# Natural token order, whole-tile stores, singly gated weights, early filler matmuls and a new order list in a gated-attention and channel-mixer kernel

## The chip, the cores and the metric

The kernel runs on one core of a Trainium2 chip. The metric is the device time in microseconds (us) of one execution. PE is TensorE, DVE VectorE, ACT ScalarE, POOL GpSimd, and SP the queue that issues loads and stores. An eviction is a copy of a result out of PSUM, the memory that PE writes to. Executions of one kernel differ here by up to 2.5% (171.99 to 176.32 us in one set of rounds), so runs marked slow (over 1.5% above the fastest of the same kernel) are left out, and ratios are taken over fast runs alone.

## The reference, cut to what matters

```python
# attention: batch 4, 8 heads, 768 tokens, head size 48; a decayed state per head
for t in range(S):
    state = alpha[:, :, t, :, None] * state + np.einsum('bhd,bhe->bhde', k[:, :, t], v[:, :, t])
    y[:, :, t] = np.einsum('bhd,bhde->bhe', q[:, :, t], state)
# then, on x = y as (4, 768, 384)
xt = x.transpose(0, 2, 1)
h = np.maximum(xt @ w_tok1, 0.0) @ w_tok2          # token mixing, 768 -> 256 -> 768
u = x + h.transpose(0, 2, 1)
h2 = np.maximum(u @ w_ch1, 0.0) @ w_ch2            # channel mixing, 384 -> 1536 -> 384
return (u + h2).astype(np.float32)
```

## The kernel before

The attention is cut into 12 steps of 256 tokens (three for each batch). A step loads alpha, k, q and v (`at`, `kt`, `qt`, `vt`, 393 KB each), builds decays by a cumulative sum of logarithms on PE, scales k and q with them (`pkk`, `pkq`), transposes both, and adds an intra-chunk part (`G`, mask, `y`) to a part from the carried state. After three steps a batch goes through the mixer: first and second token matmuls (weights `wt`), the add `u`, transposes, 24 groups of first channel matmuls with ReLU (`c1`, `rt`; weights `wc`), 24 groups of second channel matmuls (`c2`), the output add `o`, and the store. Batches overlap.

Partition p of a step holds the two tokens 2p and 2p+1, so attention comes out with even tokens ahead of odd ones. The kernel before leaves them so: the token weights are loaded and permuted to match, and each output tile is stored in two halves with rows 2 apart.

```python
    def wt2perm(self, e, stage):                       # on POOL, after the second token weight has landed
        d = self.wt2.rearrange("p k (c s t) -> p k c s t", s=2, t=64)
        s = self.natural(stage).rearrange("p k (c t s) -> p k c s t", s=2, t=64)
        for k in range(NDT):
            self.copy(e, d[:, k], s[:, k])

    def store(self, o, b, i, last):
        dst = self.out[b, i * 128 : (i + 1) * 128, :].rearrange("(t s) d -> s t d", s=2)
        for h, q in enumerate((self.nc.sync, self.nc.scalar if last else self.nc.sync)):
            q.dma_start(dst[h], self.t(o)[64 * h : 64 * h + 64, :])

    # ... weights wait for one fixed load each:
    weight("wt2", 0, 1, 786432, gates[NB - 1]["kt"], -69990.0, stage)   # k of step 2
    weight("wc2", p, 2, 1179648, gates[NB]["qt"], -69970.0 + p)         # q of step 3
```

Every operation is put on its engine in the place that a long list gives it (`ORDER`, found by a search outside the kernel); the last letter names the engine (t PE, s ACT, v DVE, g POOL, y SP):

```python
ORDER = """
ld_at0y ln0s cumw0t ld_at1y ln1s cumw1t ld_qt0y E0s IE0s ld_at3y qq0g trq0t ld_kt0y kk0v trk0t ln13s ld_qt1y
# ... cut: 839 entries in all
"""
```

Of the kernel before, what the change touches and what calls it, by code (L numbers as in the profile page):

```python
# [23 lines left out]
class Op:  # L24
    __slots__ = ("name", "eng", "prio", "preds", "vals", "emit", "mode", "idx", "start", "end", "on", "dma", "port",
                 "occ")
# [37 lines left out]
class Plan:  # L64
# [51 lines left out]
    def decode(self):  # L116
        free = {"PE": 700.0, "ACT": 700.0, "DVE": 3200.0, "POOL": 3200.0, "SP": 700.0}
# [7 lines left out]
        dma_in, dma_w, slow = 2400.0, 0.0, []  # L125
# [5 lines left out]
        for o in self.order:  # L131
            e = o.on
            occ, lat = o.eng[e]
            r = free[e]
            for p in o.preds:
                if not (e == "PE" and p.on == "PE"):
                    r = max(r, p.end)
            for v in o.vals:
# [42 lines left out]
            if o.dma is not None:  # L181
                kind, dur, lead, tail = o.dma
                if kind == "w":
                    s = max(st + lead, dma_w)
                    dma_w = s + dur
                    slow.append((s, dma_w))
                    o.end = dma_w + tail
                else:
                    dma_in = self.landed(max(st + lead, dma_in), dur)
                    o.end = dma_in + tail  # L190
            for v in o.vals:
# [20 lines left out]
W_SHARE = 0.18  # L212
B, H, S, D = 4, 8, 768, 48
HD, DT, DCH = 384, 256, 1536
NB = 3
# [13 lines left out]
def build(g):  # L229
# [6 lines left out]
    gates = {}  # L236


    def attention(n):
# [7 lines left out]

        at, kt, qt, vt = V("at"), V("kt"), V("qt"), V("vt")
        ld = {}
        for v, nm in ((at, "at"), (kt, "kt"), (qt, "qt"), (vt, "vt")):  # L250
            ld[nm] = P.op(f"ld_{nm}{n}", {"SP": (450.0, 450.0)}, -90000.0 + 10 * n, writes=[v],
                          emit=lambda e, v=v, nm=nm: g.load(nm, v, b, k), dma=("i", IN_NS, 1100.0, 650.0))
        gates[n] = ld
# [3 lines left out]
        if n in WIDE:  # L257
            lnp = O("ln", act(768, True), 0, writes=[la], reads=[at], preds=[ld["at"]], emit=lambda e: g.lnw(la, at))
            cb = V("pair")
            cum = O("cumw", pe([384] * 4 + [2] * 8), 2, writes=[cb], reads=[la], preds=[lnp],  # L260
# [4 lines left out]
        else:  # L265
# [22 lines left out]
        trk = O("trk", pe([64] * 8), 8, writes=[bk], reads=[pkk], preds=[kk], emit=lambda e: g.tr(bk, pkk), mode="R")  # L288
        trq = O("trq", pe([64] * 8), 8, writes=[bq], reads=[pkq], preds=[qq], emit=lambda e: g.tr(bq, pkq), mode="R")
        evk = O("evk", either(dve(1024, True), act(1024)), 9, writes=[tpk], reads=[bk], preds=[trk],  # L290
                emit=lambda e: g.trev(e, tpk, bk))
        evq = O("evq", either(dve(1024, True), act(1024)), 9, writes=[tpq], reads=[bq], preds=[trq],
                emit=lambda e: g.trev(e, tpq, bq))
        gtm = V("gtm")
        masks = []
        for sl in range(2):
            gp = V("pair")
            G = O(f"G{sl}_", pe([128] * 4), 10 + sl, writes=[gp], reads=[tpk, tpq], preds=[evk, evq],
                  emit=lambda e, sl=sl, gp=gp: g.gmm(gp, tpk, tpq, sl), mode="G")
            masks.append(O(f"mask{sl}_", dve(1024), 12 + sl, writes=[gtm], reads=[gp], preds=[G],  # L300
                           emit=lambda e, sl=sl, gp=gp: g.mask(gtm, gp, sl)))
        nst = 2 if k < NB - 1 else 1
        kp = V("pair")
        KO = O("K", pe([48] * 8), 9.5, writes=[kp], reads=[pkk, vb], preds=[kk, vc],
# [16 lines left out]
        yi = O("y", pe([48] * 16), 14, writes=[yp], reads=[gtm, vb], preds=masks + [vc],  # L321
# [17 lines left out]
    def weight(nm, piece, npart, bytes_, gate, prio, stage=None):  # L339
        o = P.op(f"ldw_{nm}{piece}", {"POOL": (850.0, 850.0)}, prio, preds=[gate] if gate else [],  # L340
                 writes=[stage] if stage else [], emit=lambda e: g.weight(nm, piece, gate, stage), dma=("w", bytes_ / 286.0, 2600.0, 800.0))
# [3 lines left out]
    def mixer(b):  # L345
# [4 lines left out]
        for m in range(NDT):  # L350
            bank, ht = V("one"), V("ht")
            if b == 0:
                prev = None
                for kc in range(NS):
                    o = P.op(f"t1_{b}_{m}_{kc}", pe([384]), m0 + 900 * m * sc + kc, writes=[bank], reads=[x[kc][0]],
                             preds=[x[kc][1], wl[("wt1", 0)], wl[("wt1", 1)]] + ([prev] if prev else []),
                             emit=lambda e, m=m, kc=kc, bank=bank: g.tok1(bank, m, kc, x[kc][0]))
                    prev = o
            else:
                prev = P.op(f"t1_{b}_{m}", pe([384] * 6), m0 + 900 * m * sc, writes=[bank], reads=[v for v, _ in x],  # L360
                            preds=[o for _, o in x] + [wl[("wt1", 0)], wl[("wt1", 1)]],
# [36 lines left out]
        for i in range(NS):  # L398
# [3 lines left out]
            for q4 in range(4):  # L402
                pp = []
                for mc in range(3 * q4, 3 * q4 + 3):
# [8 lines left out]
            last = b == B - 1 and i == NS - 1  # L413
            P.op(f"st_{b}_{i}", {"SP": (600.0 if last else 1180.0, 600.0)}, m0 + (16800 + 1950 * (i + 1)) * sc + hold, reads=[o_], preds=[oo],
                 emit=lambda e, i=i, o_=o_, last=last: g.store(o_, b, i, last), dma=("i", OUT_NS, 1000.0, 700.0))
# [3 lines left out]
    for p in range(2):  # L419
        weight("wt1", p, 2, 393216, gates[NB - 1]["kt"], -70000.0 + p)  # L420
    stage = V("ut")
    weight("wt2", 0, 1, 786432, gates[NB - 1]["kt"], -69990.0, stage)
    wl[("wt2", 0)] = P.op("wt2p", either({"POOL": (1700.0, 1750.0)}, {"ACT": (1650.0, 1750.0)}), -69000.0, port=True, preds=[wl[("wt2", 0)]],
                          reads=[stage], emit=lambda e: g.wt2perm(e, stage))
    for p in range(3):
        weight("wc1", p, 3, 786432, gates[NB - 1]["kt"], -69980.0 + p)
    for n in range(NB, B * NB):
        attention(n)
    for p in range(2):
        weight("wc2", p, 2, 1179648, gates[NB]["qt"], -69970.0 + p)  # L430
# [5 lines left out]
ENGINES = {"t": "PE", "s": "ACT", "v": "DVE", "g": "POOL", "y": "SP"}  # L436
ORDER = """
ld_at0y ln0s cumw0t ld_at1y ln1s cumw1t ld_qt0y E0s IE0s ld_at3y qq0g trq0t ld_kt0y kk0v trk0t ln13s ld_qt1y
ld_vt0y IE1s E1s qq1v ld_kt1y kk1g ld_vt1y evq0v evk0s G0_0t G1_0t Et1s mask0_0v vb0s K0t Et0s mask1_0v trq1t
evq1s trk1t vb1g s0_0v evk1v sa1_0v y0t ia0t fe0s G1_1t mask1_1v sm1_0g G0_1t mask0_1v ib0t x0_0v ld_at2y ln2s  # L440
cumw2t K1t E2s ld_kt2y ld_at4y P3g P4g sa0_1v x1_0s y1t ld_qt2y qq2v sm0_1v IE2s kk2v trq2t ld_vt2y vb2s ia1t
fe1s ib1t Et2s x0_1v trk2t evk2v evq2s sa1_1v lnP4s K2t G0_2t G1_2t r13s ldw_wt10g mask0_2v x1_1s ld_qt3y
ldw_wt11g t1_0_1_0t mask1_2v ldw_wt20g ld_kt3y sm1_1g q0r3g sa0_2v cum4t t1_0_0_0t t1_0_1_1t t1_0_0_1t sm0_2v
t1_0_0_2t lnP3s t1_0_0_3t k0a3v ldw_wc12g cum3t y2t ia2t fe2v ib2t x0_2s t1_0_1_2t t1_0_1_3t ldw_wc10g x1_2v
t1_0_0_4t t1_0_0_5t ht_0_0v wt2pg IE3s t1_0_1_4t E4s t1_0_1_5t ht_0_1s E3s kk3v ld_vt3y vb3s t2_0_1t u_0_1v
t2_0_0t u_0_0v IE4s ln14s ld_qt4y t2_0_5t u_0_5v ldw_wc11g t2_0_3t u_0_3v trk3t evk3s t2_0_4t u_0_4v t2_0_2t
u_0_2v ld_at5y up_0_0t ut_0_0s qq3g trq3t evq3v up_0_2t up_0_1t ut_0_1v K3t s0_3v sa1_3v G1_3t G0_3t ut_0_2s
c1_0_0_1t mask0_3v mask1_3v c1_0_0_0t c1_0_8_0t sm1_3g rt_0_0_0s r14s q0r4g ld_qt5y ld_kt4y c1_0_1_0t rt_0_1_0s
c1_0_9_1t c1_0_9_0t rt_0_0_1v c1_0_11_0t rt_0_9_1v rt_0_11_0s c1_0_3_1t c1_0_4_1t P5v lnP5s y3t ln15s qq4g ia3t
fe3s c1_0_7_1t c1_0_2_0t ld_vt4y rt_0_3_1v rt_0_4_1v r15s rt_0_7_1v rt_0_2_0s cum5t ld_kt5y ib3t rt_0_8_0s  # L450
ldw_wc20g IE5s E5s x1_3s k0a4v kk4v x0_3v c1_0_10_1t c1_0_10_0t rt_0_10_0s c1_0_11_1t c1_0_6_1t ldw_wc21g trk4t
evk4s rt_0_10_1v ld_at6y trq4t c1_0_5_1t rt_0_6_1v rt_0_11_1v c1_0_4_0t k0a5g c1_0_3_0t rt_0_3_0s rt_0_4_0s
q0r5v kk5g rt_0_5_1v evq4v c1_0_2_1t rt_0_2_1v c1_0_8_1t rt_0_8_1v qq5v c1_0_7_0t rt_0_7_0s rt_0_9_0s c1_0_6_0t
rt_0_6_0s c1_0_1_1t rt_0_1_1v trk5t evk5v trq5t c1_0_5_0t G1_4t vb4s K4t sa0_4v c2_0_2_0t sm0_4g mask1_4v
rt_0_5_0s sa1_4v sm1_4v c2_0_4_0t c2_0_4_1t ld_vt5y vb5g evq5s ld_at9y G0_5t G0_4t mask0_4v c2_0_3_0t mask0_5v
c2_0_1_0t c2_0_2_1t c2_0_2_2t c2_0_3_1t G1_5t K5t sa0_5v c2_0_3_2t c2_0_4_2t ld_at7y ln17s r17s c2_0_1_1t
c2_0_1_2t c2_0_1_3t ln16s P6v mask1_5v lnP6s P7v sm0_5v y5t o_0_1v y4t ld_qt6y ia4t ld_at8y P8g ld_qt7y ld_vt7y
lnP7s ia5t fe5v fe4v P9g c2_0_3_3t o_0_3v ib5t x1_5v ib4t x1_4v cum7t c2_0_2_3t q0r7v ld_vt6y x0_5s c2_0_4_3t
cum6t E7s ld_kt7y x0_4s t1_1_1t r16s lnP9s ld_kt6y ht_1_1v st_0_3y st_0_1y t1_1_0t c2_0_0_0t c2_0_5_0t ln18s
IE7s E6s ht_1_0s t2_1_5t t2_1_3t q0r6v ld_qt9y ld_at11y ld_vt8y qq7v IE6s ln19s o_0_2v qq6v t2_1_1t u_1_3v  # L460
u_1_1v c2_0_5_1t c2_0_5_2t t2_1_0t st_0_2y t2_1_2t c2_0_0_1t vb6g c2_0_5_3t u_1_2v up_1_1t k0a6g kk6g t2_1_4t
u_1_0v up_1_0t r19s u_1_5v lnP8s u_1_4v c2_0_0_2t k0a7g c2_0_0_3t up_1_2t ut_1_1s vb7s kk7g ut_1_0v c1_1_2_0t
o_0_4v o_0_5v rt_1_2_0v K6t ut_1_2v ld_vt9y trq7t evq7s c1_1_0_0t s0_6v o_0_0v sa1_6v c1_1_11_0t rt_1_11_0v
rt_1_0_0v c1_1_4_0t rt_1_4_0v c1_1_3_1t ld_kt8y ld_at10y rt_1_3_1s c1_1_1_0t rt_1_1_0v st_0_0y c1_1_8_0t
rt_1_8_0v trq6t evq6s trk6t evk6v trk7t c1_1_5_1t rt_1_5_1s sm1_6v evk7v c1_1_6_0t K7t G1_6t vb8s sa0_7v sm0_7v
c1_1_3_0t c1_1_1_1t rt_1_1_1s ld_kt10y rt_1_6_0v sa1_7v c1_1_6_1t rt_1_6_1s r18s P10g sm1_7g mask1_6v cum9t IE9s
cum8t c1_1_7_1t IE8s rt_1_7_1s c1_1_5_0t ld_kt11y E9s c1_1_9_0t ld_qt8y q0r8g E8s ln110s c1_1_4_1t c1_1_7_0t
# [416 lines left out]
```

## Time and profile before

| stretch of the profiled execution | us | what limits it |
|---|---|---|
| front, to the first channel matmul | 38.3 | loads and weights, one after another |
| dense part, to the last output add | 132.9 | PE, idle for 1.3 us |
| tail, last output add and last store | 4.2 | one store after one add |
| span | 175.4 | |
| time of a run | 178.06 median (177.62 to 178.57) | |

The slices, the stretches and the chain of waits are shown and read in the prediction. The stretches are read thus: us of the stretch, then busy us (and instructions) of PE, PEld (weight load), DVE, ACT and POOL, then the granted clock, the share of the DMA engines and GB/s. One more view of the kernel before is needed later: what DVE and PE waited for between 90 and 110 us (who waited for whom; total us, times, longest):

```profile
DVE o L831 <- DMA out_dram<-o: 2.8, 2, 2.2
PEld L634 <- DVE o L831: 1.2, 1, 1.2
PE ps L634 <- DVE o L831: 0.8, 1, 0.8
```

Output adds stand waiting for a free output buffer, which an earlier store still holds, and PE stands waiting for the adds.

### The profile page before, as it was taken

How to read it: one execution, taken by the hardware profiler on the slowest of the kernel's cores; microseconds unless marked ns; L12 is line 12 of the kernel's file. 1: busy time of each engine (PE TensorE's matmuls, PEld its weight loads, DVE VectorE, ACT ScalarE, POOL GpSimd, SP SyncE). 2: the span in 40 equal slices, each digit the busy share in tenths (PEclk: the TensorE clock that was granted, in tenths of full speed). 3: DMA queues.
4: the chain of work that ended last, by engine and by line, in shares of the span. 5: the costliest groups of instructions: out<-in, count | busy, mean ns of one | idle time of the engine just before them, and what ended most of it. 6: DMA issues, size and time to landing. Idle time of an engine off the chain costs nothing.

```text
span 175.4 us, 5752 instructions
## 1 busy us (share of the span) xinstructions
PE 157.1 (90%) x2489; PEld 100.4 (57%) x2489; DVE 122.3 (70%) x224; ACT 78.7 (45%) x154; POOL 52.9 (30%) x62
## 2 busy tenths in 40 slices
PE   0748849799999999999999989999999999999990
PEld 0337645476656566666566556666666666666650
DVE  4058948799998869898787588987995256354321
ACT  3874470767763566357824352564432211323100
POOL 5227806735743042923350807053010000000000
PEclk9999999999999999999999999999999999999998
DMA  5999999996999998989601646303000100331153
GB/s 144 322 324 300 261 221 257 232 258 168 280 204 256 271 313 205 302 217 285 156 4 29 162 101 175 87 0 93 4 4 5 43 0 2 90 93 45 40 142 87
DMA packets 57625, 27.11 MB, mean 155 GB/s; under 512 B 50816, under 2 KB 57600, under 8 KB 57600
## 3 DMA queue, kind: packets, MB, share of 16 engines
q1 hardware_dynamic: 53680, 23.50, 51.6%
q0 software_dynamic: 3840, 3.15, 11.5%
q8 instruction: 19, 0.31, 0.7%
q10 hardware_dynamic: 80, 0.10, 0.3%
q14 instruction: 6, 0.05, 0.1%
HBM read 25.17 MB, written 4.72 MB: 170 GB/s over the span
## 4 chain that ended last, share of the span: by engine, by line
PE 69%; DMA 12%; SPq 9%; DVE 3%; issue 2%; POOL 2%; ACT 1%; DVEq 0%; POOLq 0%
PE ps L827 25%; PE ps L822 21%; PE ps L634 8%; SPq L581 8%; PE ps L798 5%; PE ps L803 5%; DMA wt<-in_moe_w_tok_dram 4%; DMA qt<-in_q_dram 3%; DMA at<-in_alpha_dram 3%; PE ps L814 2%; PE ps L690 2%; DMA out_dram<-o 2%; SPq L614 2%; DVE o L831 1%; DVE rt L795 1%
## 5 line engine op out<-in xcount | busy, mean ns | idle before, releaser
L827 PE MATMUL ps<-wc,rt 128*128 128x384 bf16 x288 | 52.7, 326 | 0.0
L822 PE MATMUL ps<-ut,wc 128*128 128x384 bf16 x288 | 51.3, 326 | 0.1
L822 PEld LDWEIGHTS <-wc 128*128 128x128 bf16 x288 | 26.9, 98 | 17.5 <-issue 0.3
L827 PEld LDWEIGHTS <-rt 128*128 128x128 bf16 x288 | 26.8, 98 | 16.9
L793 ACT ACTIVATE rt<-ps 128x384 bf16<-128x384 f32 x48 | 22.1, 491 | 28.7 <-PE ps L822 25.5
L795 DVE TENSOR_SCALAR rt<-ps 128x384 bf16<-128x384 f32 x48 | 24.9, 551 | 9.1 <-PE ps L822 8.9
L725 DVE TENSOR_TENSOR gtm<-ps,mk 128x1024 bf16<-128x1024 f32 x24 | 28.5, 1216 | 3.4 <-PE ps L634 2.3
L831 DVE TENSOR_TENSOR o<-ps,u 128x384 f32<-128x384 f32 x24 | 13.1, 552 | 11.5 <-PE ps L827 8.7
L675 POOL TENSOR_TENSOR pkq<-qt,E 128x768 bf16<-128x768 f32 x7 | 12.7, 1813 | 8.3 <-ACT E L659 4.8
L754 POOL TENSOR_TENSOR ss<-tmp,E 128x192 bf16<-128x192 f32 x9 | 4.6, 508 | 32.1 <-DVE tmp L751 31.0
L807 DVE TENSOR_TENSOR u<-ps,x 128x384 bf16<-128x384 f32 x24 | 11.9, 550 | 2.3 <-PE ps L803 2.1
L675 DVE TENSOR_TENSOR pkk<-kt,IE 128x768 bf16<-128x768 f32 x8 | 7.6, 955 | 6.6 <-POOL pkq L675 6.4
L634 PE MATMUL ps<-la,u 128*128 128x384 bf16 x18 | 6.7, 443 | 6.0 <-ACT la L628 5.2
L634 PE MATMUL ps<-tpq,tpk 48*64 48x128 bf16 x384 | 9.7, 242 | 1.5 <-ACT tpk L711 1.1
L798 PE MATMUL ps<-x,wt 128*128 128x384 bf16 x48 | 9.9, 349 | 0.5 <-DMA wt<-in_moe_w_tok_dram 0.4
L711 ACT COPY ut<-ps 128x768 bf16<-128x768 bf16 x6 | 4.8, 798 | 11.3 <-PE ps L814 11.2
L803 PE MATMUL ps<-ht,wt 128*128 128x384 bf16 x48 | 9.3, 326 | 0.6 <-ACT ht L793 0.6
L711 ACT CAST x<-ps 128x384 bf16<-128x384 f32 x12 | 5.7, 483 | 8.9 <-PE ps L634 8.9
L634 PEld LDWEIGHTS <-tpk 48*64 48x64 bf16 x384 | 7.1, 121 | 4.2 <-issue 2.4
L619 POOL TENSOR_TENSOR at<-at 128x384 f32<-128x384 f32 x6 | 5.9, 999 | 10.9 <-DVE ss L754 10.3
L675 POOL TENSOR_TENSOR pkk<-kt,IE 128x768 bf16<-128x768 f32 x4 | 7.3, 1813 | 5.2 <-DMA kt<-in_k_dram 3.4
L711 ACT COPY tpk<-ps 128x1024 bf16<-128x1024 bf16 x7 | 7.1, 1014 | 2.7 <-PE ps L690 2.7
(76 smaller groups left out, 199.4 us busy)
## 6 DMA issues: line engine op xcount, KB each, us to landing
at<-in_alpha_dram SPq DMA_DIRECT2D x12, 384.0 KB, 5.5
qt<-in_q_dram SPq DMA_DIRECT2D x12, 384.0 KB, 5.5
kt<-in_k_dram SPq DMA_DIRECT2D x12, 384.0 KB, 5.1
vt<-in_v_dram SPq DMA_DIRECT2D x12, 384.0 KB, 5.2
out_dram<-o SPq DMA_DIRECT2D x47, 96.0 KB, 2.4
wc<-in_moe_w_ch_dram POOLq DMA_DIRECT2D x3, 384.0 KB, 7.7
wc<-in_moe_w_ch_dram POOLq DMA_DIRECT2D x2, 576.0 KB, 9.2
wt<-in_moe_w_tok_dram POOLq DMA_DIRECT2D x2, 192.0 KB, 6.5
```

The source lines that it names most:

```text
L581: self.ins[id(v)] = self.nc.sync.dma_start(self.t(v), src)
L634: return self.pe.matmul(out, lhsT=lhsT, rhs=rhs, start=start, stop=stop, skip_group_check=True)
L675: self.shared(self.eng[e].tensor_tensor(self.t(dst)[:, :, :, 0:D], self.t(src).rearrange("p h s d -> p s h d"), bass.AP(tensor=f.tensor, o ...
L711: return self.act.copy(d, s)
L725: self.nc.vector.tensor_tensor(self.t(gtm)[:, sl, :, :], self.pair(gp).rearrange("p a (j t) -> p (a j) t", t=128), bass.AP(tensor=m.tensor ...
L793: self.act.activation(d, s, AF.Relu)
L795: self.nc.vector.tensor_scalar_max(d, s, 0.0)
L798: self.pe.matmul(self.bank(bank)[:, 0:HD], lhsT=self.wt1[:, kc, m * 128 : m * 128 + 128], rhs=self.t(x), start=(kc == 0), stop=(kc == NS - 1))
L803: self.pe.matmul(self.bank(bank)[:, 0:HD], lhsT=self.wt2[:, kc, i * 128 : i * 128 + 128], rhs=self.t(hts[kc]), start=(kc == 0), stop=(kc = ...
L822: self.pe.matmul(self.bank(bank)[:, 0:HD], lhsT=self.wc1[:, kc, mc * 128 : mc * 128 + 128], rhs=self.t(ut)[:, kc, half * 384 : half * 384 ...
L827: self.pe.matmul(self.bank(bank)[:, 0:HD], lhsT=self.t(rts[mc][0])[:, i * 128 : i * 128 + 128], rhs=self.wc2[:, mc, :], start=(mc == 0), s ...
L831: self.nc.vector.tensor_tensor(self.t(o), self.bank(bank)[:, 0:HD], self.t(u), ALU.add)
```

## The change

Its intent: turn the tokens back into natural order once, where q's transposes are evicted, so that weights need no permutation and stores are whole; let each weight wait for the last load that the order puts ahead of it; fill PE's early idle time with matmuls on zeros; and search a new order for all this.

```diff
+    def trevq(self, e, d, bp):                         # q eviction: two-byte elements, step 2
+        self.copy(e, self.t(d).rearrange("p f j (t s) -> p f s (j t)", s=2),
+                  self.pair(bp).bitcast(BF16)[:, :, 0:512].rearrange("p f (s c) -> p f s c", s=2))
-    def wt2perm(self, e, stage):
-        ...
-    def store(self, o, b, i, last):
-        dst = self.out[b, i * 128 : (i + 1) * 128, :].rearrange("(t s) d -> s t d", s=2)
-        for h, q in enumerate((self.nc.sync, self.nc.scalar if last else self.nc.sync)):
-            q.dma_start(dst[h], self.t(o)[64 * h : 64 * h + 64, :])
+    def store(self, o, b, i):
+        self.nc.sync.dma_start(self.out[b, i * 128 : (i + 1) * 128, :], self.t(o))
+    def fill(self, bank, count):
+        for _ in range(count):
+            self.mm(self.bank(bank)[:, 0:192], self.zs[:, 0:128], self.zs, True, True)
@@ weights
-    for p in range(2):
-        weight("wt1", p, 2, 393216, gates[NB - 1]["kt"], -70000.0 + p)
+    weight("wt1", 0, 786432, -70000.0)                 # gate: the last load ahead of it in the order
@@ ORDER, as a whole (cut)
-ld_at0y ln0s cumw0t ld_at1y ln1s cumw1t ld_qt0y E0s IE0s ld_at3y qq0g trq0t ld_kt0y kk0v trk0t ln13s ld_qt1y
+... ld_at0y ln0s ... f0trq_0t f1cumw_1t ... ld_at1y ln1s f2cumw_1t ld_qt0y ... cumw0t E0s ld_kt0y ...
```

Masks and one layout in PSUM change with the token order and are cut here (the product with the mask takes 1,216 ns before and 1,218 after). The order list also moves work: 64 ReLU evictions on ACT and 32 on DVE (48 and 48 before), and more of the elementwise products on POOL.

## The prediction

> **What bounds the kernel now.** I read the page's slices first, for where TensorE (PE) is not busy; then busy time by stretch, to turn that into microseconds; then the chain that ended last, to see what holds each stretch back; then the timeline of the front for the cause. The slices:
>
> ```profile
> PE   0748849799999999999999989999999999999990
> PEclk9999999999999999999999999999999999999998
> DMA  5999999996999998989601646303000100331153
> ```
>
> A slice is 4.39 us. PE has holes in the first eight slices (to about 35 us) and in the last; in between it is full. The DMA engines are the reverse: full to about 80 us, then nearly free. By stretch (columns: busy us of PE, PEld, DVE, ACT, POOL, then clock, DMA share, GB/s):
>
> ```profile
> 0.00:27.20 27.20, 15.38 (x405) 11.76 (x406) 15.14 (x32) 15.49 (x26) 12.49 (x23) 1.00 1.06 260
> 27.20:38.30 11.10, 10.11 (x197) 6.52 (x198) 9.13 (x18) 6.23 (x11) 5.91 (x7) 1.00 1.19 250
> 38.30:171.20 132.90, 131.61 (x1893) 82.12 (x1889) 97.45 (x175) 56.98 (x117) 34.54 (x33) 1.00 0.52 127
> 171.20:175.40 4.20, 0.00 (x1) 0.00 (x0) 0.56 (x1) 0.00 (x0) 0.00 (x0) 0.88 0.35 84
> ```
>
> The span is thus 38.3 us of front, 132.9 us dense (idle 1.29 us), and 4.2 us of tail (last output add, last store). VectorE (DVE) is busy 97 of the dense 133 us, so it does not bind there. The time is set by when the dense part starts, and the chain says what that start waits for:
>
> ```profile
> 12.90 5.75 DMA at<-in_alpha_dram
> 18.65 0.07 issue
> 18.72 1.00 POOL at L619
> 19.73 0.78 POOL wt L599
> 20.50 6.55 DMA wt<-in_moe_w_tok_dram
> 27.05 0.14 issue
> ...
> 33.52 1.46 PE ps L803 x8
> ...
> 38.34 4.49 PE ps L822 x27
> ...
> 163.40 7.81 PE ps L827 x48
> 171.22 0.02 issue
> 171.24 0.56 DVE o L831
> ```
>
> POOL stands in line behind a product that needs the 12th load, only then issues the first token weight (two half loads), which lands at 27.05. The timeline adds two facts:
>
> ```profile
> 27.93 1.76 PE L798 MATMUL ps<-x,wt 128*128 128x384 bf16 x5
> 30.15 0.56 DVE L667 TENSOR_TENSOR kt<-kt,at 128x384 f32<-128x384 f32 x1 [0.63 <-DMA kt<-in_k_dram]
> 30.77 1.59 POOL L712 COPY wt<-ut 128x768 bf16<-128x768 bf16 x2 [1.78 <-DVE kt L667]
> 38.28 4.56 PE L822 MATMUL ps<-ut,wc 128*128 128x384 bf16 x27
> ```
>
> Five 384-column matmuls take 1.76 us at 28 us (about 0.32 us apart), 27 take 4.56 us at 38 us (0.163 apart): PE runs at half rate through the front although the granted-clock row reads 9. And a k load issued at 18.63 landed only at 30.15: weights in flight starve the loads.
>
> [...] 3,840 software-queue packets carry 3.15 MB (820 B each), 53,680 of the SP queue 23.50 MB (438 B)[...]. The q eviction now writes with step 2[...]: today's 686 ns for 1024 elements becomes, as an estimate from the fp32-source mask over the same 1024 (1,216 ns), some 1.2 us. No trace yet shows the strided form.
>
> **The change, part by part.**
>
> 1. *No weight permutation.* Two POOL copies (1.59 us) after the second token weight go, and the staging wait with them. They ended at 32.36; the second token matmuls started at 33.52, after the hidden eviction, so alone this frees 0 us; it matters only once the rest moves up.
>
> 2. *q eviction.* I count 6 on DVE (7 before), 6 on ACT (5). DVE: 6 × (1.2 − 0.69) = +3 us, which is more than offset by the new order: ReLU evictions 32 on DVE (48 before), 16 × 0.551 = −8.8 us, and 64 on ACT, 16 × 0.491 = +7.9 us on an engine busy 45%. Not on the path; only one eviction, of attention step 2, lies in the front (+0.5 us).
>
> 3. *Loads and weights.* New load order: all of step 2 is among the first 13 loads (before: 14, with its v, the 14th, caught behind weights until 23.1). The first token weight waits for the 12th load, as in effect before, but POOL no longer does the step-4 product first. By hand, loads land every 1.25 us from 5.5 us (2nd) to 18.5 (12th). POOL's query product of step 2 runs 16.8 to 18.6; the weight issues at about 18.7 instead of 19.7, as one transfer, and lands at about 25.5 (6.8 us later; before, 7.4 over two issues): −1.5 us. The second token weight waits for the 13th load and POOL's state products: issue about 22.3, landing about 29 (6.5 to 8 us). The first channel weight waits for the 15th load (about 25.2): issue 26, landing about 33.4 (7.7 median).
>
> 4. *Front on the other engines.* Step 0 starts with the query product on DVE (0.95 us) instead of POOL (1.81), and ACT takes step 2's logarithm earlier (about 13 instead of 16.6). Step 2's x is ready about 28 (32.1 before), the hidden evictions about 29.6 (33.5), and 4.2 us of token matmuls, adds and transposes later (4.8 before, when a q eviction stood in DVE's way) comes the first channel matmul: 33.8 from this side, 33.4 from its weight. I take 34.2 against 38.3: **−4.1 us**.
>
> 5. *Fillers.* 30 matmuls of 192 columns on zeros: 22 run before the first cumulative sum, at 0.165 us cold, 3.6 us, from about 1.4 to 5.0; the first logarithm ends at 5.15. So they delay nothing. If they warm the clock, step-0 to step-2 matmuls halve, and the 12 token matmuls save 12 × 0.16 = 1.9 us. Most of that is hidden, as the weights' landing holds the front; it is included in the 34.2.
>
> 6. *Dense part.* The same matmuls. Adding up the list after the first channel matmul in both orders with warm spacings gives 132.5 against 132.1 us. The 1.29 us of idle lies in 80 to 110, behind the SP queue where pairs of stores (about 1.1 us of issue each) stand before loads; one store each halves this: −0.5. With PE 4 us ahead and the DMA engines full, some new wait on a load or weight is likely: +0.5.
>
> 7. *Tail.* Last add 0.56 us, one store of 192 KB in place of two halves issued from two queues: ±0.2.
>
> Sum −4.1 − 0.5 + 0.5 = −4.1 us: 178.06 becomes 174.0.
>
> **Rivals.** (a) *The DMA engines take it back.* They are full to 80 us; the second channel weights (gated on k of steps 4 and 5) must be in when the second channel matmuls start, about 14.7 us after the first: 48.9 instead of 53.1. Needed by then from HBM: 20 loads (7.9 MB) and 5.1 MB of weights, 13.0 MB. Before, about 27 loads and 3.9 MB were in at 52.6, some 14.6 MB; at that rate 13.0 MB plus half a megabyte running ahead is there at about 49. So it just fits, because the new order holds back steps 6 and later. If it doesn't, 2 to 3 us of the gain are lost: 176 to 177. (b) *The fillers don't warm the clock, or it cools again.* For: two cold stretches of busy PE before 27 us did not warm it. Cold, the token matmuls cost 1.9 us more, of which about 1 shows: 175. If warmth does count on the path of steps 0 to 2, where it may save up to 2 us, the front ends nearer 33: 172.5. (c) *ACT or POOL becomes the bound,* with 16 more ReLUs, and about 9 us more products on POOL. Both are under 55% busy after the addition; POOL's product takes 1.81 us against 0.95, so single chains get longer: 175 at worst.
>
> **Range and chances.** The front's start is the large term, uncertain by ±1.5 us; new waits in 40 to 85 us from 0 to 3. So 171.3 to 177.2. The 2% line is 174.5, close above my number; both halves of the error count: faster 0.57, same 0.40, slower 0.03. Slower would need a stall of 7 us, which nothing here suggests.
>
> **What would show it.** The first token weight landing near 25.5; the first channel matmuls at 34.2; PE dense from there, 132 to 134 us; tail near 4.2; 384-column spacing in the front 0.163 if warm; the q eviction on DVE near 1.2 us. I am wrong if the first channel matmul starts after 36.5, or if PE is idle over 3 us between 40 and 90 us waiting on weights or loads.

## The result, and the profile after

The changed kernel took 173.29 us (median of 4 runs, 172.94 to 174.21) against 178.24 us (177.62 to 178.57) of the kernel before. The ratio is 0.973, with a 95% interval of 0.969 to 0.978: faster, inside the stated range and on the side that the chances favoured. A ratio here is the mean time of one kernel's fast runs over that of the other's of the same rounds, so it is not quite the ratio of the medians. The profiled executions are 175.4 and 171.2 us long.

The slices of the changed kernel:

```profile
PE   7759679999989899999999999999999999999992
PEclk9995555999999999999999999999999999999999
DMA  5999999999999519999999410021000021120123
```

PE is now full from the seventh slice on, and a new thin place lies at the twelfth to fourteenth (47 to 60 us). The clock row, which read 9 through the whole front before, now reads 9 for three slices, 5 for four, and 9 again: the granted clock was 0.50 from 12.2 to 29.3 us. The same stretches, cut at the first channel matmul and the last output add:

```profile
0.00:34.99 34.99, 28.27 (x599) 20.75 (x599) 22.43 (x41) 22.88 (x40) 17.87 (x29) 0.76 1.08 257
34.99:45.00 10.01, 9.95 (x140) 6.14 (x138) 7.91 (x13) 7.58 (x17) 4.25 (x5) 1.00 1.10 244
45.00:60.00 15.00, 13.75 (x239) 8.23 (x238) 8.87 (x15) 7.68 (x16) 5.43 (x6) 1.00 1.03 216
60.00:110.00 50.00, 49.98 (x893) 32.40 (x892) 39.82 (x71) 30.99 (x64) 29.16 (x24) 1.00 0.67 188
110.00:167.90 57.90, 57.87 (x658) 35.89 (x656) 30.85 (x54) 19.98 (x43) 5.10 (x5) 1.00 0.13 46
167.90:171.20 3.30, 0.00 (x0) 0.00 (x0) 0.56 (x1) 0.00 (x0) 0.00 (x0) 1.00 0.32 119
```

The front fell from 38.28 to 34.99 us, the dense part is 132.91 us (132.96 before), the tail fell from 4.16 to 3.30: −3.29 − 0.05 − 0.86 = −4.20 us. PE's idle time in the dense part did not shrink, it moved: 1.25 us now lie between 45 and 60 us and almost nothing between 60 and 110, where the kernel before lost 1.29 us.

The chain of work in the front (start, duration, what):

```profile
12.68 5.98 DMA kt<-in_k_dram
18.66 0.30 issue
18.97 7.57 DMA wt<-in_moe_w_tok_dram
...
26.59 1.14 PE ps L810 x3
...
28.00 2.21 PE ps L810 x9
...
30.79 2.11 PE ps L815 x12
...
35.15 0.97 PE ps L834 x6
```

The first token weight waits for its gate, the 12th load, and not for POOL; the permutation is gone; the first token matmuls (L810) still run at less than full rate (three take 1.14 us and nine 2.28, against 0.66 and 1.64 in the run warmwc2), and from the second ones (L815) to the first channel matmul (L834) it is 4.2 us. What PE waited for between 35 and 70 us is one thing alone, the second channel weights:

```profile
PE ps L839 <- DMA wc<-in_moe_w_ch_dram: 1.2, 2, 0.6
```

### The profile page after: what moved, and what is told of

It reads as the page before. It is cut to its first block, busy times and chain, and to the rows that moved or that the text cites. A ratio compares the mean times of both kernels' runs of the same rounds, so it can differ in the third digit from the quotient of the medians.

```text
span 171.2 us, 5785 instructions
## 1 busy us (share of the span) xinstructions
PE 159.8 (93%) x2519; PEld 103.4 (60%) x2519; DVE 110.4 (64%) x191; ACT 89.1 (52%) x178; POOL 61.8 (36%) x68
## 3 DMA queue, kind: packets, MB, share of 16 engines
HBM read 25.17 MB, written 4.72 MB: 175 GB/s over the span
## 4 chain that ended last, share of the span: by engine, by line
PE 76%; DMA 13%; SPq 7%; ACT 1%; issue 1%; DVE 0%; POOL 0%
PE ps L834 26%; PE ps L839 26%; PE ps L637 9%; SPq L599 7%; DMA wc<-in_moe_w_ch_dram 6%; PE ps L810 5%; PE ps L815 5%; DMA wt<-in_moe_w_tok_dram 4%; DMA kt<-in_k_dram 3%; PE ps L826 2%; PE ps L698 2%; ACT tpq L723 1%; DVE o L843 0%; POOL ss L766 0%
## 5 line engine op out<-in xcount | busy, mean ns | idle before, releaser
L834 PE MATMUL ps<-ut,wc 128*128 128x384 bf16 x288 | 51.5, 326 | 0.1
L805 ACT ACTIVATE rt<-ps 128x384 bf16<-128x384 f32 x64 | 28.7, 500 | 25.2 <-PE ps L834 24.9
L834 PEld LDWEIGHTS <-wc 128*128 128x128 bf16 x288 | 27.3, 98 | 17.8 <-issue 0.3
L737 DVE TENSOR_TENSOR gtm<-ps,mk 128x1024 bf16<-128x1024 f32 x24 | 28.7, 1218 | 3.7 <-PE ps L637 3.7
L807 DVE TENSOR_SCALAR rt<-ps 128x384 bf16<-128x384 f32 x32 | 16.8, 552 | 8.4 <-PE ps L834 8.4
L682 POOL TENSOR_TENSOR pkq<-qt,E 128x768 bf16<-128x768 f32 x9 | 16.3, 1813 | 13.2 <-DMA qt<-in_q_dram 7.2
L766 POOL TENSOR_TENSOR ss<-tmp,E 128x192 bf16<-128x192 f32 x12 | 6.1, 507 | 17.7 <-DVE tmp L763 14.4
L723 ACT CAST x<-ps 128x384 bf16<-128x384 f32 x17 | 7.4, 482 | 8.4 <-PE ps L637 8.4
L682 POOL TENSOR_TENSOR pkk<-kt,IE 128x768 bf16<-128x768 f32 x6 | 10.9, 1819 | 2.0 <-ACT IE L663 2.0
L810 PE MATMUL ps<-x,wt 128*128 128x384 bf16 x48 | 9.8, 355 | 0.1
L815 PE MATMUL ps<-ht,wt 128*128 128x384 bf16 x48 | 9.1, 326 | 0.0
L723 ACT COPY tpk<-ps 128x1024 bf16<-128x1024 bf16 x8 | 8.1, 1019 | 0.9 <-PE ps L698 0.8
L678 POOL TENSOR_TENSOR qt<-qt,lf 128x384 f32<-128x384 f32 x7 | 7.0, 1001 | 4.5 <-ACT lf L634 2.9
L763 DVE TENSOR_TENSOR tmp<-ps,ss 128x192 f32<-128x192 f32 x16 | 5.7, 355 | 4.5 <-PE ps L637 2.7
L723 ACT COPY tpq<-ps 128x1024 bf16<-128x1024 bf16 x6 | 7.9, 1309 | 0.8 <-PE ps L698 0.8
```

Of the source, the lines that this page charges most:

```text
L682: self.shared(self.eng[e].tensor_tensor(self.t(dst)[:, :, :, 0:D], self.t(src).rearrange("p h s d -> p s h d"), bass.AP(tensor=f.tensor, o ...
L723: return self.act.copy(d, s)
L737: self.nc.vector.tensor_tensor(self.t(gtm)[:, sl, :, :], self.pair(gp).rearrange("p a (j t) -> p (a j) t", t=128), bass.AP(tensor=m.tensor ...
L805: self.act.activation(d, s, AF.Relu)
L807: self.nc.vector.tensor_scalar_max(d, s, 0.0)
L810: self.pe.matmul(self.bank(bank)[:, 0:HD], lhsT=self.wt1[:, kc, m * 128 : m * 128 + 128], rhs=self.t(x), start=(kc == 0), stop=(kc == NS - 1))
```

## The experiments

All of them were run with timed rounds beside the kernel before, and each has one profile. The table sums them up; front, dense and tail are read from the profile, as above. The last column is over fast runs. There were three sets of rounds, on three chips: again, nofill, evqplain and splitst; then oldorder, permnew, wc2early and warmwc2; then splitlast, splitfirst, best and again2. Each set has its own runs of the kernel before, but the second has none of the changed kernel, so its ratios can be set beside the changed kernel's only across sets.

| run | front | dense | tail | span | ratio (95%) |
|---|---|---|---|---|---|
| kernel before | 38.28 | 132.96 | 4.16 | 175.4 | 1 |
| changed kernel | 34.99 | 132.91 | 3.30 | 171.2 | 0.973 (0.969 to 0.978) |
| again | 36.23 | 132.85 | 3.32 | 172.4 | 0.972 (0.967 to 0.977) |
| nofill | 35.76 | 132.08 | 3.36 | 171.2 | 0.971 (0.966 to 0.976) |
| evqplain | 35.27 | 132.59 | 3.34 | 171.2 | 0.975 (0.969 to 0.980) |
| splitst | 34.97 | 132.82 | 4.61 | 172.4 | 0.986 (0.979 to 0.993), 3 of 6 runs |
| oldorder | 40.90 | 133.62 | 3.38 | 177.9 | 1.010 (1.003 to 1.017) |
| permnew | 35.88 | 133.96 | 4.16 | 174.0 | 0.989 (0.981 to 0.996) |
| wc2early | 35.44 | 132.74 | 3.32 | 171.5 | 0.977 (0.972 to 0.982) |
| warmwc2 | 35.48 | 133.45 | 3.37 | 172.3 | 0.983 (0.977 to 0.988) |
| splitlast | 35.91 | 132.57 | 4.72 | 173.2 | 0.982 (0.977 to 0.987) |
| splitfirst | 39.39 | 131.90 | 3.71 | 175.0 | 0.984 (0.977 to 0.990) |
| best | 35.55 | 132.14 | 3.31 | 171.0 | 0.965 (0.957 to 0.973), 3 of 6 runs |
| again2 | 35.78 | 132.84 | 3.38 | 172.0 | 0.969 (0.965 to 0.974) |

My theory: the new order, through the time at which the weights land, makes the front shorter; the whole-tile store makes the tail shorter; fillers and evictions matter little. Rivals: warmth from the fillers, the token order and the gates themselves, or issue work on SP in the middle.

**The changed kernel repeated (again, again2).** No edit.

> The changed kernel itself, as the yardstick of this chip: 173.3 us by all theories, within 0.5%; first channel matmul near 35.1 us, PE idle near 1.2 us between 50 and 57 us waiting for the second channel weights.

> The changed kernel once more, as yardstick for the three runs beside it: 172.5 to 173.5 us, ratio 0.970 to 0.975; tail 3.3 us; first channel matmul 35.0 to 36.3 us, moving with the landing of the first token weight (26.5 to 27.1 us in the profiles so far).

Measured: medians 172.88 and 173.30 us, ratios 0.972 and 0.969. The first channel matmul came at 36.23 and 35.78 us, against 34.99 in the first profile of the very same program, and the tail at 3.32 and 3.38. The tail agrees within 0.1 us in these three, and the front scatters by over 1 us between executions: differences of that size between two fronts say nothing from one profile each.

The three profiles show what makes up this scatter. The first token matmul starts at 26.59, 26.85 and 27.25 us, and the nine that follow it in one group take 2.28, 3.06 and 2.44 us, as the granted clock comes back up in the middle of them (at about 29.3 us in the first profile) or only after them (at about 32 us in again, whose granted clock is 0.63 over 26 to 34 us). The remainder up to the first channel matmul is 6.1 to 6.3 us in all three. The chains differ too: in the first profile the front's chain runs through the first token weight; in again and again2 there is no weight in it, only attention work of DVE, ACT and PE. So two chains of nearly equal length end in the token matmuls, and either can be the later one.

**Without fillers (nofill).**

```diff
-f0G1_0t ... f0trq_0t f1cumw_1t ... f2cumw_1t ... f0K_0t ... f0K_2t
+f0G1_0n ... f0trq_0n f1cumw_1n ... f2cumw_1n ... f0K_0n ... f0K_2n     # n: not emitted
```

> The changed kernel without its 30 filler matmuls. Theory A (the fillers warm the clock from 5.3 to 12.8 us only, and the front then waits for the first token weight at 26.5 anyway): the front runs cold, step 0 is later by about 1 us, the first channel matmul moves by less than 0.5 us, time +0.0 to +0.5 us. Rival B (warmth in steps 0 to 2 carries the gain of the front): first channel matmul 1.5 to 2.5 us later, time +1.5 us or more.

Measured: ratio 0.971 against 0.972 of the run beside it. The first channel matmul came at 35.76 us, inside the scatter of the front, and PE's idle time between 45 and 60 us was 0.17 us instead of 1.25. Theory A holds: the fillers are worth nothing that these runs can see beside the scatter. In the changed kernel the clock comes up after them, as its timeline of PE shows:

```profile
1.09 3.70 PE L637 MATMUL ps<-zs 128*128 128x192 bf16 x22 [1.09 <-DVE zs L567]
5.08 0.78 PE L637 MATMUL ps<-la,u 128*128 128x384 bf16 x3 [0.29 <-ACT la L631]
...
13.64 1.12 PE L637 MATMUL ps<-la,u 128*128 128x384 bf16 x3 [0.17 <-ACT la L631]
```

22 fillers run to 4.8 us; three matmuls of 384 columns then take 0.78 us, and the same three at 13.6 us take 1.12. By the granted clock, full rate lasts from 5.4 to 12.2 us and is gone when the token matmuls come (0.50 from 12.2 to 29.3 us).

**The strided eviction (evqplain).** The result is wrong on purpose: the tokens of q stay in the old order.

```diff
-        self.copy(e, self.t(d).rearrange("p f j (t s) -> p f s (j t)", s=2), ...)
+        self.copy(e, self.t(d).rearrange("p f j t -> p f (j t)"), self.pair(bp).bitcast(BF16)[:, :, 0:512])
```

> The changed kernel with the q eviction writing with step 1 again, so tokens are in the wrong order in the intra-chunk part and the result is wrong on purpose. It measures what the strided write costs. Expected: eviction back from 1,304 to 690 ns on DVE and from 1,309 to 1,010 ns on ACT, 6 of each, so 3.7 and 1.8 us less busy. Theory A (these engines have slack): time -0.0 to -0.4 us. Rival B (the evictions of steps 0, 2, 3 and 4 lie on the chain, as the chain's 1.32 us piece at 43.1 us suggests): time -0.6 to -1.2 us.

Groups of instructions (busy us, mean ns of one), first the changed kernel, then this run:

```profile
L723 ACT COPY tpq<-ps 128x1024 bf16<-128x1024 bf16 x6 | 7.9, 1309 | 0.8 <-PE ps L698 0.8
L724 DVE COPY tpq<-ps 128x1024 bf16<-128x1024 bf16 x6 | 7.8, 1304 | 0.5 <-PE ps L637 0.5
```

```profile
L722 ACT COPY tpq<-ps 128x1024 bf16<-128x1024 bf16 x6 | 6.1, 1016 | 0.8 <-PE ps L698 0.8
L723 DVE COPY tpq<-ps 128x1024 bf16<-128x1024 bf16 x6 | 4.1, 682 | 0.5 <-PE ps L637 0.5
```

The step of two costs 622 ns on DVE and 293 ns on ACT for each eviction, 5.5 us of engine time in all, and the time did not move (ratio 0.975 against 0.972 beside it). Theory A holds: taking 0.3 us out of the eviction on ACT that stood in the chain at 43 us did not shorten the run by an amount that shows.

**The order list under the new code (oldorder), and under the old code (permnew).**

```diff
 # oldorder: the changed code
-ORDER = the new list
+ORDER = the list of before, without the second half weight and the permutation; fillers not emitted
 # permnew: the code of before
-ORDER = the list of before
+ORDER = the new list without fillers; the second half weight and the permutation put back on POOL
```

> The code of the changed kernel (natural order, whole-tile stores, weights gated singly, no permutation) with the order list of the kernel before, without fillers. Theory A (the new order gives the shorter front, the whole-tile store the shorter tail): first channel matmul still near 38 us, tail from the last add 3.3 us instead of 4.2, time 1 to 2 us under the kernel before, ratio 0.989 to 0.995. Rival B (token order and gates are what count, the order is a detail): first channel matmul near 35.5, ratio 0.975 to 0.98.

> The code of the kernel before (permuted weights, half stores, fixed gates) with the order list of the change, without fillers, with the second half weight and the permutation put back into POOL's list. Theory A: most of the front's gain is there (first channel matmul 35.5 to 37), the tail stays at 4.2 us or more, and half stores cost issue time in the middle: ratio 0.98 to 0.99. Rival B: first channel matmul near 38 again, ratio 0.995 or more.

oldorder was the surprise: not 1 to 2 us faster, but 1.0% slower than the kernel before. Its tail is short, as expected (3.38), and its front is 40.90 us, longer than any other. The chain of waits of this run shows the place:

```profile
15.18 5.91 DMA vt<-in_v_dram
21.09 0.30 issue
21.39 7.70 DMA wt<-in_moe_w_tok_dram
```

In the old list the last load ahead of the first token weight is the 14th, v of step 2, while the kernel before let it wait for the 11th, by name. The weight goes out at 21.39 instead of 19.73 us and lands at 29.09 instead of 27.05. Later in the same chain stands a q eviction on DVE, 1.32 us at 38.96, right before the first channel matmuls. So by the chain the new gating rule costs time unless the order is searched with it. (The runs do not take the gate and the eviction apart here; the chain names both.) permnew, the counterpart, has the front at 35.88 us with the old gates, the permutation and no fillers: of the front's gain, all that exceeds the scatter comes with the order. Its tail is the old 4.16 us. Theory A holds for permnew, and Rival B falls in both. (The mean granted clock of permnew's front is 0.76, as in the changed kernel, although it has no fillers; nofill's front is as short, and its first token matmuls ran at half rate, three in 1.14 us and nine in 2.61.)

permnew also answers for the permutation. Its chain enters the second token matmuls (L803) through the two copies on POOL, which wait for the second token weight:

```profile
30.22 1.60 POOL wt L712 x2
31.86 2.00 PE ps L803 x11
```

PE stands for 0.42 us waiting for the copies alone. In the old order the permutation was over before it was needed; in the new one it ends last, so leaving it out is worth something, though no run measures how much by itself.

**Split stores (splitst, splitlast, splitfirst).** Each output tile is stored in two halves of 64 partitions, both from SP: all tiles, those of the last batch, or those of the first three.

```diff
-        self.nc.sync.dma_start(self.out[b, i * 128 : (i + 1) * 128, :], self.t(o))
+        for h in range(2):                       # splitlast: if b == 3, splitfirst: if b < 3
+            self.nc.sync.dma_start(self.out[b, i * 128 + 64 * h : i * 128 + 64 * h + 64, :],
+                                   self.t(o)[64 * h : 64 * h + 64, :])
```

> The changed kernel with each output tile stored in two halves of 64 partitions again, both from the SP queue. Theory A (the whole-tile store is what shortened the tail from 4.2 to 3.3 us): tail from the start of the last output add back to 4.1 us or a little more (the last tile of the kernel before used two queues), time +0.8 to +1.1 us; the dense part unchanged within 0.3 us. Rival B (the tail is shorter for another reason, such as the SP queue having been behind at the end): tail stays at 3.3 us, time +0.2 us or less. Rival C (halved issue work on SP also feeds the loads earlier): more than 1.5 us slower, with new PE idle between 65 and 100 us.

> The changed kernel with the stores of the last batch alone split in halves on the SP queue. Theory A (the tail and the middle both cost): tail 4.6 us as with all stores split, time +1.0 to +1.5 us over the changed kernel, no waits of the output adds for stores. Rival C (the whole loss of 3.6 us lies in the middle): +0.3 us or less.

> The changed kernel with the stores of batches 0 to 2 split and the last batch whole. Theory A: tail 3.3 us, and output adds or loads wait behind the longer SP queue between 65 and 110 us; time +1.5 to +2.5 us over the changed kernel. Rival (the tail alone costs, and the rest of the 3.6 us was scatter): +0.3 us or less.

The tail answers clearly: 4.61 and 4.72 us where the last batch is split, 3.71 in splitfirst, whose last batch is whole, and 3.30 to 3.38 in the runs with whole stores throughout. The SP queue at the end shows the issue part of it, in the kernel before and in the changed one:

```profile
171.82 1.11 SPq L614 DMA_DIRECT2D out_dram<-o  x2
```

```profile
168.49 0.33 SPq L617 DMA_DIRECT2D out_dram<-o  x1
```

Two halves take 1.11 us to issue and a whole tile 0.33; from issue to landing a half takes 2.4 us (median) in the kernel before and 2.2 in splitst, permnew and splitfirst, and a whole tile 1.9 in the changed kernel, again, again2, best and splitfirst. The whole tile, though it is twice the bytes, is the quicker one in both parts. For the last tile the issue is most of it: 0.78 of the 0.86 us by which the tail of the changed kernel is shorter. In splitst and splitlast the tail is longer still, as SP has a half of the tile before to issue first (three issues, to 169.9 and 170.6 us).

The times say more than the tails: splitst's ratio is 1.4 points above again's, some 2.5 us, with a tail longer by 1.29. splitlast's ratio is 1.3 points above again2's, some 2.3 us, with a tail longer by 1.34. And splitfirst, whose last batch is whole, is 1.4 points above, some 2.6 us. Rival C would put that into the middle, but no profile shows it there: PE is idle for 0.27 us between 60 and 120 us in splitst and also in splitfirst, the one run of these in which output adds wait for stores is splitst (1.0 us, hidden from PE), and the dense parts are as long as without splits. splitfirst's profile has instead a front of 39.39 us, before any store, although its instructions up to there are those of the changed kernel: the k load that is the first weight's gate landed at 20.6 us and the weight took 8.9 us. Whether such fronts are more frequent in these programs, or fell there by chance, cannot be told from six runs each; the timed runs leave no trace. So about 1 us in the tail is shown (0.9 to 1.4, by which unsplit tail one takes), and the rest of what splitting costs stays open.

**The wait for the second channel weights (wc2early).** In the five profiles so far with the new order and the new code, the last output add started 111 to 112 us after the second of these weights had landed. This run issues both earlier.

```diff
-... ldw_wc11g ... ld_vt3y ... vb3g ... ld_at5y P5g ld_kt4y ... ldw_wc20g ... k0a4g ... ld_kt5y ... sm1_3g ... ldw_wc21g
+... ldw_wc11g ... ld_vt3y ... ld_at5y ld_kt4y ldw_wc20g vb3g ... P5g ... k0a4g ... ld_kt5y ldw_wc21g ... sm1_3g
```

> The changed kernel with the two second channel weights issued earlier on POOL: the first right after the third first-channel weight's successor in line (before the v cast of step 3 and the product of step 5), the second right after the k product of step 4. Nothing else moves, the loads keep their order. Theory A (after the first channel matmul, the end is anchored by the landing of the second of these weights at 56.7 us: in five profiles the last output add starts 111 to 112 us after that): PE no longer waits 1.2 us there, the last add starts 0.8 to 1.2 us earlier, time -0.7 to -1.2 us against the changed kernel. Rival B (the DMA engines are the limit, weights that come earlier push loads later): new PE idle of the same size waiting on v, q or k, time within 0.4 us of the changed kernel.

The wait is gone (PE waits for no weight after 35 us), and PE's idle time between 45 and 60 us fell from 1.25 to 0.84 only: 0.7 us of it is now a transpose group that waits for an eviction of x on DVE. The dense part is 132.74 us, against 132.84 to 132.91 in three profiles of the changed kernel, and the ratio 0.977 is no better than the changed kernel's. (The forecast gain, 0.4 to 0.7%, is about as large as the interval of ±0.5%, so it is the profile that speaks here.) A fixed distance to a late event is no proof that the event holds the end: everything after it was simply PE work in a fixed order. Theory A's gain did not come; Rival B's new idle time did in part, though what came up was not the loads it named.

**A warm front (warmwc2, best).** 13 more groups of fillers ahead of the matmuls of steps 0 to 2, on top of wc2early; in best the second token weight is besides issued right behind the first.

```diff
-trq0t ... trk0t ... K0t ... trk1t ... cumw2t ... G1_1t ... y0t ... K1t ... trq2t ... trk2t ... G0_2t ... G1_2t ... y2t
+f1trq_0t trq0t ... f0trk_0t trk0t ... f1K_0t K0t ... f0trk_1t trk1t ... f0cumw_2t cumw2t ...   # and so on
 # best, besides:
-ldw_wt10g sm0_1g ... vb2g sm1_1g ldw_wt20g
+ldw_wt10g ldw_wt20g sm0_1g ... vb2g sm1_1g
```

> As the run before, and 13 more groups of filler matmuls (4 or 6 each) ahead of the matmuls of steps 0 to 2, so that the clock should stay up from 5 us until the token matmuls. Theory A (the front waits for weights, not for PE; but with the later anchor gone, the token matmuls run warm and bring the first channel matmul to about 34): spacing of the 384-column token matmuls 0.163 us, first channel matmul 0.8 to 1.3 us earlier, time 0.3 to 1 us under the run before. Rival B (the weights' landing holds everything): first channel matmul earlier but the time the same within 0.3 us.

> The run with more fillers and earlier second channel weights, with the second token weight besides issued directly behind the first (it waited for the state product of step 1, and in that run landed at 31.3 us and held the second token matmuls). Theory A (the front is bound by the landing of the weights, one after another): second token matmuls start near 30 instead of 31.3 us, first channel matmul 34.0 to 34.5 instead of 35.5, time 0.8 to 1.3 us under that run, at or under the changed kernel. Rival B (the loads pushed back by it, k and q of step 3, hold the next weights, which wait for that q): first channel matmul within 0.4 us of 35.5 or a new idle of the same size after it, time within 0.4 us of that run.

The clock stayed up: in warmwc2 the token matmuls run at full rate. The timeline of PE:

```profile
28.10 0.66 PE L810 MATMUL ps<-x,wt 128*128 128x384 bf16 x3 [1.22 <-DMA wt<-in_moe_w_tok_dram]
28.90 1.64 PE L810 MATMUL ps<-x,wt 128*128 128x384 bf16 x9
31.34 2.12 PE L815 MATMUL ps<-ht,wt 128*128 128x384 bf16 x12 [0.23 <-DMA wt<-in_moe_w_tok_dram]
```

Nine take 1.64 us where they took 2.28. But PE stands idle for 1.22 us ahead of them, waiting for the first token weight, and for 0.23 us ahead of the second: the first channel matmul comes at 35.48 us all the same. From the first token matmul to the first channel matmul it is 7.38 us here and 7.21 in best, against 8.40 to 9.38 in the three profiles of the changed kernel, so the warm clock does shorten that stretch by 1 us or more. What took it back is the weight: the k load that is its gate landed at 19.6 and 20.3 us in these two profiles, against 18.7 to 19.0, and the first token matmul came at 28.10 and 28.34 us. Whether the fillers cause that or chance does cannot be told from two profiles. Theory A falls, and Rival B is not met either: the first channel matmul was not earlier, and the six runs are longer than wc2early's (medians 175.17 and 174.13 us; the intervals of the ratios overlap). Nor did the clock stay up everywhere: the mean granted clock was 1.000 in the profiled run, the fastest of the six, and 0.980 to 0.990 in the other five.

best put the second token weight ahead of the loads of step 3 and began the channel matmuls at 35.55 us, so my theory of the weights standing in a row falls in this form as well: the first weight landed at 28.3 us there, and moving the second behind it did not show. Its three fast runs average 172.6 us, and three more took 175.1 to 175.9; over all six the median is 173.94 against 173.30 of again2. The three longer ones are those in which the granted clock fell (0.987 to 0.990, against 0.997 to 1.000); no profile shows where. I do not call it an improvement. None of the experiments beats the changed kernel with certainty.

## Why the prediction was right

The number was right: −4.1 us predicted, −4.2 us between the two profiles, −4.95 us between the medians. That it came out so well is luck: in the first profile the front fell 0.8 us short of its term, and the tail gave 0.86 us more than its.

1. *What bounds the kernel* was right. Front plus dense part plus tail describe every run above. The dense part stays within 131.9 to 134.0 us whatever was edited, a range of 2.1 us beside 5.9 us for the front and 1.4 for the tail. One reading was too wide: "PE runs at half rate through the front" holds to about 31 us only. At 32.13 us four token matmuls of the kernel before take 0.81 us and at 33.52 us eight take 1.46, which is 0.163 apart, so full rate was back before the first channel matmul. That loads land late while weights are in flight is in both traces: in the kernel before, loads with no weight in flight landed 3.5 to 5.9 us after their issue and the eight issued from 16.23 to 31.30 us, with weights in flight, 6.9 to 13.5; in the changed kernel it is 3.4 to 6.7 us, and 8.4 to 14.8 for the seven issued from 17.43 to 32.95. How the DMA engines are shared between the two was not shown: no run isolates it.
2. *Permutation* (step 1) and *eviction* (step 2): the permutation was off the path in the kernel before, as said, and "it matters only once the rest moves up" came true: permnew has it on its chain, so it belongs to the gain, by an amount not measured. The eviction is off the path. The estimate of 1.2 us for the strided form was low by 0.1 (1,304 ns on DVE), and I had not thought that ACT would pay too (1,309 instead of 1,011 ns). evqplain shows that neither matters.
3. *Loads and weights* (step 3): the 12th load and the issue at 18.7 us came out as worked out (18.66 and 18.97); the landing was put at 25.5 and was at 26.54, as the one large transfer took 7.57 us and not 6.8. The first channel weight's issue was put at 26 and was at 26.16.
4. *The front* (step 4) was the term that was too large: −4.1 predicted, −3.29 in the first profile, −2.05 and −2.50 in its two repeats (36.23 and 35.78 against 38.28). In the first profile the late landing, 1.04 us, covers the whole shortfall of 0.8. In the repeats it is the engines that are later, and step 5, "If they warm the clock", whose gain I counted into the 34.2: nine token matmuls took 2.28 us in the first profile, 3.06 in again and 1.64 at full rate in warmwc2. The 4.2 us from the second token matmuls to the channel matmuls was met exactly in the first profile.
5. *Fillers* (step 5): 3.6 us from 1.4 to 5.0 was predicted, 3.70 us from 1.09 to 4.79 measured, and full rate from 5.4 us. The rate was lost again at 12.2 us. That the fillers raise the clock was my estimate: in the trace the rise comes after them, and what raises or lowers the clock was not shown. "12 × 0.16 = 1.9 us" fits twelve matmuls that all run cold, as in again (1.14 + 3.06 us, against 0.66 + 1.64 in warmwc2); in the kernel before only the first six did. That "most of that is hidden" agrees with nofill, whose time does not differ; that the weights alone hide it is not shown, as in again and again2 no weight ends the front.
6. *Dense part* (step 6): −0.5 and +0.5 were put down; in fact −1.27 (the idle time of 80 to 110 us went from 1.29 to 0.02) and +1.25 (the wait for the second channel weights, at the place that rival (a) named). The signs and the sum were right, the sizes were not. That the SP queue's shorter issue is what removed the first is not shown by itself: splitst and splitfirst have little idle time there either (0.25 and 0.07 us). But permnew, with halves under the new order, has 1.09 us there, and oldorder, with whole stores under the old one, 0.79 us and no output add that waits for a store (2.8 us in the kernel before). So the stores end those waits, and which part of the change ends PE's idle time stays open.
7. *Tail* (step 7): "±0.2" was the step that failed. It was −0.86. I had weighed two halves issued from two queues against one store and taken them as equal; for the last tile the halves were both on SP (the two-queue store belongs to tile 5, which the order does not put last), and two halves take 1.11 us to issue where a whole tile takes 0.33; that is 0.78 of the 0.86. splitlast and splitst confirm the direction at 4.72 and 4.61 us.

Of the rivals, (a) came true in small, (b) came true as to cooling, at a price that varies (up to 0.8 us of the nine token matmuls, again against the first profile), (c) did not: ACT is busy for 52% and POOL for 36%.

## What to carry to other kernels

Split a profile into front, dense part and tail before working out a change, and give the tail the same care as the front: here the last store's issue and landing were worth a microsecond, and one store of all 128 partitions beat two of 64 (tails of 3.30 to 3.71 us against 4.16 to 4.72). An ordering rule such as "wait for the last load ahead of me" is good or bad only together with the order it is applied to; test the two apart, as oldorder and permnew do. Where two chains of nearly equal length end in the same place, as the weight and the attention work do here, shortening one shows little. A wait seen at a thin place of a busy engine is not yet a gain: remove it and look at what fills its place.

## What the traces show besides

- A reading of 1.00 of the granted clock went here with half rate as well as with full rate: the kernel before reads 1.00 in every stretch from 0 to 38.3 us, and ran its 384-column matmuls 0.32 us apart at 28 us and 0.163 apart at 32 us. In the changed kernel the reading is 1.00 up to 5.4 us too, where 22 fillers of 192 columns took 3.70 us, 0.16 us apart, and four more took 0.49 us at 9.90 us, 0.08 apart.
- The q eviction of 1,024 two-byte elements out of PSUM took 682 ns on DVE with step 1 and 1,304 with step 2, and 1,016 and 1,309 ns on ACT.
- A store of 64 partitions (96 KB) took SP some 0.6 us to issue and landed in 2.2 to 2.4 us; one of 128 partitions (192 KB) took 0.36 us and landed in 1.9 (medians).
- The transfers of the same program scatter: with the same instructions up to there, the DMA engines moved 205 to 265 GB/s between 18.5 and 26 us, and the first channel matmul came at 34.97 to 39.39 us.
